# A gated recurrence and a dense block: when the weights of the second layer are converted, and where a unit's pairs stand

## The chip, the cores and the metric

The kernel runs on one core of one Trainium2 chip. The metric is the device time of one execution in microseconds (us); less is better. Engines are named as the profile names them: PE is TensorE (PEld its weight loads), DVE is VectorE, ACT is ScalarE, POOL is GpSimd, SP is SyncE, which only issues transfers here.

## The reference

For 4 batches and 8 heads, a recurrence over 768 steps with a 48x48 complex state, and then a dense block with a squared ReLU on 3072 rows of 384:

```python
mag = np.sqrt(a_re * a_re + a_im * a_im)
scale = np.minimum(mag, 0.999) / (mag + 1e-06)
a_re_n, a_im_n = (a_re * scale, a_im * scale)
for t in range(S):
    ar, ai = (a_re_n[:, :, t, :, None], a_im_n[:, :, t, :, None])
    new_re = ar * S_re - ai * S_im
    new_im = ar * S_im + ai * S_re
    kv = np.einsum('bhd,bhe->bhde', k[:, :, t], v[:, :, t])
    S_re, S_im = (new_re + kv, new_im)
    y[:, :, t] = np.einsum('bhd,bhde->bhe', q[:, :, t], S_re)
...
x = y.transpose(0, 2, 1, 3).reshape(B * S, H * D)
h = x @ w_in            # 384 -> 2048
r = np.maximum(h, 0.0)
out = (r * r) @ w_out   # 2048 -> 384
```

## The kernel before, in words

The work is cut into 8 units: each of the 4 batches in two halves of 384 steps. The second half of a batch takes over the state of the first. A unit goes through four stages.

- **Chain** (chain_work: load, roots, normalise, inner, inverse, totals, scan, back, apply). The decays are normalised and their products over time formed, mostly on DVE with some steps on ACT. Each step works on the 8 heads in two halves, z = 0 and z = 1 (4 heads each). Three steps need PE: totals turns the last products round (tile tot, L770), and after the scan back turns the results round again (tile bk, L835); apply then multiplies q and k by them and writes the tile QK (L862). The K half of QK goes to DRAM and back (rows, L869; KC, L871) to get another layout. These transfers are issued by POOL, and so are the loads of units 2 to 7 (L643); the loads of units 0 and 1 are issued by SP.
- **Pairs** (pair_work: turn, keep, score, mix). For each of 4 pairs of heads: transposes of QK (tq, L890), copied by ACT (QKT, L891); products of k and v (kv, L917), which DVE adds up to states (St, S, L925 and L927); scores (sa, L900), which DVE masks (A, L902); and the outputs (ypair, L936 and L941), which ACT copies to yt (L944) and SP sends to their place in xT (L952).
- **First dense layer** (hidden, L971): 16 tiles h of 128x384, three matmuls each; each matmul is two records in the trace. ACT makes g of h in two operations (L976, L977). The tiles h and o have three PSUM buffers together.
- **Second dense layer** (project, L985): three tiles o with 16 matmuls each, copied by ACT and stored by SP (L991).

The weights arrive as 64-bit floating-point numbers and are converted in 32 pieces of 128x384, 16 of w_in (tile w1) and 16 of w_out (w2). fetch (L581) loads a raw piece; lower (L589, ACT) scales its low words; convert (L602, L606, L609, DVE) makes the 32-bit numbers, frees the buffer and fetches another piece. The raw pieces of w2 have five buffers. The first five are fetched by POOL at the start, the other eleven by SP, each when a buffer comes free. `after(x, y)` puts an instruction behind another in the order and adds no wait on a semaphore. The first operation of a conversion is put so behind a QK: of unit 0 for w1 and the first five pieces of w2, of unit 1 for the other eleven.

The order of the program is written out by hand at the end of fast_path: lists of steps are either run one after the other or merged, each list spread evenly over the merged one. A scheduler then sets the order of instructions on each engine from this order and the dependencies, and each engine runs its instructions in that order. The order of stages is:

1. the chain of unit 0, with the first fetches in it;
2. the pairs of unit 0, merged with the conversions of w1;
3. the fetches of five pieces of w2; then the chain of unit 1, then the first layer of unit 0;
4. the pairs of unit 1, merged with the conversions of w2; then the chain of unit 2;
5. for n = 1 to 7: both dense layers of unit n, merged with the pairs of unit n+1 and the chain of unit n+2. For n = 1 the second dense layer of unit 0 is put ahead of unit 1's. In the last two, checks of the inputs take the place of the chain.

At the end a flag is read; for inputs out of range a second, general path would run, which these inputs don't take.

Of the kernel before, what the change touches and what calls it, by code (L numbers as in the profile page):

```python
# [481 lines left out]
def fast_path(ctx, tc, q, k, v, a_re, a_im, moe_w_in, moe_w_out, out, flag):  # L482
# [21 lines left out]
    NF = FF // C  # L504
# [12 lines left out]
    NRAW = 5  # L517
# [9 lines left out]
    def after(x, y):  # L527

        tc.add_manual_dep(x.ins, y.ins.name, NOSYNC, reason="order")
# [14 lines left out]
    mark = {}  # L544
# [13 lines left out]
    def piece(i):  # L558
        words = 2 if wide else 1
        if i < NF:  # L560
            w_in = moe_w_in.bitcast(U32) if wide else moe_w_in
            return (w1[:, i].rearrange("p m f -> p (m f)"),
                    w_in[:, ts(i, words * C)].rearrange("(m p) f -> p m f", p=C))
        i -= NF
        w_out = moe_w_out.bitcast(U32) if wide else moe_w_out
        return w2[:, i], w_out[ts(i, C), :].unsqueeze(1)
# [4 lines left out]
    def fetch(i):  # L571

        dst, src = piece(i)
        if not wide:
            nc.gpsimd.dma_start(
                out=dst.rearrange("p (m f) -> p m f", m=src.shape[1]), in_=src)
            return

        raw = raws[i] = (gp.tile([C, DM, 2], U32, name="raw", tag="g") if i < NF else
                         wst.tile([C, DM, 2], U32, name="raw", tag="raw"))  # L580
        get = (nc.sync if i >= NF + NRAW else nc.gpsimd).dma_start(  # L581
            out=raw.rearrange("p (m f) two -> p m (f two)", m=src.shape[1]), in_=src)
        after(get, mark["landed"])

    def lower(i):

        if wide:
            lo = raws[i][:, :, 0]
            op = act.activation(out=lo, in_=lo, func=AF.Copy, scale=2.0 ** -29)  # L589
            after(op, mark["last"])  # L590

    def convert(i):

        for j in range(i, i + AHEAD) if i % NF == 0 else [i + AHEAD - 1]:
            if j // NF == i // NF:
                lower(j)
        if wide:
            dst, _ = piece(i)
            more, hi = raws[i][:, :, 0], raws[i][:, :, 1]
            bits = dst.bitcast(U32)  # L600

            first = dve.tensor_scalar(out=bits, in0=hi, scalar1=0x07FFFFFF, scalar2=3,  # L602
                                      op0=ALU.bitwise_and, op1=ALU.logical_shift_left)

            after(first, mark["QK", int(i >= NF + NRAW)])
            dve.scalar_tensor_tensor(out=bits, in0=hi, scalar=0xC0000000, in1=bits,  # L606
                                     op0=ALU.bitwise_and, op1=ALU.bitwise_or)

            dve.tensor_tensor(out=bits, in0=bits, in1=more, op=ALU.add)  # L609
        n = i + (NF // 2 if i < NF else NRAW)  # L610
        if n < (NF if i < NF else 2 * NF):
            fetch(n)
# [44 lines left out]
    def flat(t):  # L657
        return t.rearrange("p h c d -> p (h c d)")
# [86 lines left out]
    def measure_rest(u):  # L745
        for z in range(2):
            measure(u, 4 + z, whole(u["qk", z]))
        measure(u, 6, u["v"].rearrange("p j h d -> p (j h d)"))
# [90 lines left out]
    def apply(u, z):  # L839

        a, fa, fb, hs = u["a", z], u["fa", z], u["fb", z], ts(z, HH)
        xn, qk = u["xn"], u["qk", z]

        def over(j):
            return xn[:, j, hs].unsqueeze(2).to_broadcast([C, HH, W, D])

        dve.tensor_tensor(out=qk[:, 1], in0=qk[:, 1], in1=over(2), op=ALU.mult)
        for j, f in ((0, fa), (1, fb)):
            for r in range(2):
                dve.tensor_tensor(out=f[:, r], in0=a[:, r], in1=over(j), op=ALU.mult)  # L850
        dve.tensor_tensor(out=flat(a[:, 0]), in0=flat(fa[:, 0]), in1=flat(fb[:, 1]),
                          op=ALU.subtract)
        dve.tensor_tensor(out=flat(a[:, 1]), in0=flat(fa[:, 1]), in1=flat(fb[:, 0]),
                          op=ALU.add)
        t = pr.tile([C, 2 * HH * W * R], F32, name="QK", tag="QK")
        half = HH * W * R
        out_q = u["Q", z] = t[:, 0:half].rearrange("p (h c e) -> p h c e", h=HH, c=W)
        out_k = t[:, half:2 * half].rearrange("p (c h e) -> p c h e", h=HH, c=W)
        u["K", z] = out_k
        for j, o in ((1, out_k.rearrange("p c h e -> p h c e")), (0, out_q)):  # L860
            for r in range(2):
                done = dve.tensor_tensor(out=o[:, :, :, r * D:(r + 1) * D], in0=qk[:, j],  # L862
                                         in1=a[:, r], op=ALU.mult)
        mark["QK", u["n"]] = done

        rows = dram.tile([L, HH * R], F32, name="rows", tag=f"rows{z}")
        kc = u["KC", z] = nat.tile([C, NM, HH, R], F32, name="KC", tag=f"KC{z}")
        n = NM - u["half"]
        nc.gpsimd.dma_start(out=rows.rearrange("(p c) e -> p (c e)", c=W),  # L869
                            in_=out_k.rearrange("p c h e -> p (c h e)"))  # L870
        nc.gpsimd.dma_start(out=kc[:, 0:n].rearrange("p j h e -> p j (h e)"),  # L871
                            in_=rows.rearrange("(j p) e -> p j e", p=C)[:, 0:n])
# [7 lines left out]
    def turn(u, i, c):  # L880

        if c == 0:
            u.setdefault("T", {})[i] = pr.tile([R, 4, L], F32, name="QKT", tag="QKT")
        z = 2 * i // HH
        ps = bank(u, [R, 4, C], "tq", c == 1)
        for j in range(2):
            for h in range(2):
                hh = (2 * i + h) % HH
                src = u["K", z][:, c, hh] if j else u["Q", z][:, hh, c]
                nc.tensor.transpose(ps[:, 2 * j + h], src, ident)  # L890
        act.copy(out=u["T"][i].rearrange("r z (p c) -> r c z p", c=W)[:, c], in_=ps)  # L891
# [63 lines left out]
    def pair_work(u):  # L955
        w = []
        for i in range(NP):
            w += [[lambda i=i, c=c: turn(u, i, c)] for c in range(W)]
            if i:
                w += [[lambda i=i: keep(u, i - 1)], [lambda i=i: score(u, i, 0)],  # L960
                      [lambda i=i: mix(u, i - 1)], [lambda i=i: score(u, i, 1)]]
            else:
                w += [[]] + [[lambda h=h: score(u, 0, h)] for h in range(2)]
        w += [[lambda: keep(u, NP - 1)], [], [lambda: mix(u, NP - 1)], [], []]
        return [lambda fs=fs: [f() for f in fs] for fs in w]
# [27 lines left out]
    def hidden_work(u):  # L993
        return [lambda f=f: hidden(u, f) for f in range(NF)]

    def project_work(u):
        return [lambda c=c, p=p: project(u, c, p) for c in range(W) for p in range(4)]

    def chain_work(u):
        def both(*fs):  # L1000
            return [lambda z=z, f=f: f(u, z) for f in fs for z in range(2)]

        return ([lambda: load(u), lambda: None, lambda: None] + both(roots, normalise, inner, measure_roots, inverse)
                + [lambda j=j: totals(u, j) for j in range(3)]
                + [lambda: scan(u), lambda: measure_rest(u)]
                + [lambda j=j: back(u, j) for j in range(3)] + both(apply))
# [28 lines left out]
    def merge(*lists):  # L1035

        order = sorted((((i + 0.5) / len(w), n, i) for n, w in enumerate(lists)
                        for i in range(len(w))))
        for _, n, i in order:
            lists[n][i]()  # L1040

    units = [{"b": b, "half": half, "n": b * NHALF + half}
             for b in range(B) for half in range(NHALF)]
# [3 lines left out]
    merge(pair_work(units[0]), [lambda i=i: convert(i) for i in range(NF)])  # L1047
    for i in range(NF, NF + NRAW):
        fetch(i)
    for f in chain_work(units[1]) + hidden_work(units[0]):  # L1050
        f()
    merge(pair_work(units[1]), [lambda i=i: convert(i) for i in range(NF, 2 * NF)])
    for f in chain_work(units[2]):
        f()
    for n in range(1, NU):
        u = units[n]
        lists = [hidden_work(u) + project_work(u)]
        if n == 1:
            lists[0] = project_work(units[0]) + lists[0]
        if n + 1 < NU:  # L1060
            lists.append(pair_work(units[n + 1]))
        if n + 2 < NU:
            lists.append(chain_work(units[n + 2]))
        elif n + 1 < NU:
            lists.append([lambda i=i: inspect(i) for i in range(2 * NF)])
        else:
            lists.append([verdict])
        merge(*lists)
# [53 lines left out]
```

## Time and profile before

| what | value |
|---|---|
| median of 9 runs | 807.94 us (801.63 to 814.22) |
| the profiled execution's own time | 810.44 us |
| its span, first to last instruction | 808.6 us |
| mean granted PE clock in it | 0.969 of full speed |
| busy time of PE, DVE, ACT, POOL | 710.4, 518.9, 398.1, 109.9 us |
| HBM read, written | 56.62 MB, 14.16 MB |

Times in the profile are counted from the first instruction. A line of the order in time has the start, the time, the engine, the line of the kernel, the operation, the tiles out<-in, the shape and the count of instructions merged in it, and in brackets how long the engine was idle before it and what ended that. Each instruction's time overlaps a little with the next one's, so the distance from start to start is what counts. A matmul's time includes its way through the array.

### The profile page before, as it was taken

What the parts mean: (1) busy time and instruction counts of PE and PEld (TensorE: products, weight loads), DVE (VectorE), ACT (ScalarE), POOL (GpSimd) and SP (SyncE); (2) the same over time, 40 slices, a digit from 0 to 9 for tenths busy, and PEclk for the clock granted to TensorE, in tenths of its full rate; (3) what the DMA queues carried; (4) which work ended last, traced back from release to release, by engine and by line L of the source; (5) the groups of instructions that cost most, each with busy time, mean ns of one, the idle gap of its engine ahead of it and who ended that gap; (6) DMA issues with size and microseconds to landing.
All of it is one profiled execution on the core that took longest, in us unless ns stands there. A gap on an engine that the chain in (4) does not pass through costs nothing.

```text
span 808.6 us, 9895 instructions
## 1 busy us (share of the span) xinstructions
PE 710.4 (88%) x3474; PEld 463.8 (57%) x3474; DVE 518.9 (64%) x1332; ACT 398.1 (49%) x753; POOL 109.9 (14%) x162
## 2 busy tenths in 40 slices
PE   0138895599899999999999998999999999899997
PEld 0027553475466566666666665666666665566554
DVE  5897799987988985549582867378655957500000
ACT  5824495355478519931685139711982145212510
POOL 5003100410030023000500041002200144100000
PEclk9996898699999999999999999999999999899999
DMA  9428320551042035000800052003500278500000
GB/s 282 147 73 272 105 78 20 177 183 53 11 166 84 18 95 176 9 18 18 277 12 7 28 191 71 13 14 114 184 9 18 76 242 268 185 17 28 1 12 23
DMA packets 38747, 76.24 MB, mean 94 GB/s; under 512 B 10752, under 2 KB 25216, under 8 KB 38688
## 3 DMA queue, kind: packets, MB, share of 16 engines
q0 software_dynamic: 14608, 55.85, 21.3%
q1 hardware_dynamic: 24080, 19.67, 8.2%
q8 instruction: 29, 0.48, 0.2%
q14 instruction: 30, 0.25, 0.1%
HBM read 56.62 MB, written 14.16 MB: 88 GB/s over the span
## 4 chain that ended last, share of the span: by engine, by line
PE 28%; issue 27%; DVE 13%; DMA 10%; ACT 8%; POOL 2%; SPq 0%; POOLq 0%; ACTq 0%
PE o L985 15%; PE h L971 6%; DMA a<-in_a_im_dram 3%; DMA rows<-QK 2%; DVE fa L799 2%; DMA look<-in_moe_w_in_dram 2%; DMA look<-in_moe_w_out_dram 2%; PE sa L900 2%; DVE fa L706 2%; ACT QKT L891 1%; DVE a L694 1%; PE ypair L941 1%; PE ypair L936 1%; ACT g L976 1%; DVE QK L862 1%
## 5 line engine op out<-in xcount | busy, mean ns | idle before, releaser
L971 PE MATMUL h<-xT,w 128*128 128x384 f32 x768 | 269.1, 492 | 4.6 <-DMA xT<-yt 3.1
L985 PE MATMUL o<-w,g 128*128 128x384 f32 x768 | 264.9, 493 | 0.0
L985 PEld LDWEIGHTS o<-w,g 128*128 128x128 f32 x768 | 141.4, 192 | 85.7 <-issue 4.9
L971 PEld LDWEIGHTS h<-xT,w 128*128 128x128 f32 x768 | 139.0, 192 | 83.6 <-issue 6.2
L891 ACT COPY QKT<-tq 96x512 f32<-96x512 f32 x96 | 79.9, 855 | 36.0 <-PE tq L890 36.0
L976 ACT ACTIVATE g<-h 128x384 f32<-128x384 f32 x128 | 61.5, 484 | 54.8 <-PE h L971 54.7
L890 PE MATMUL tq<-ident,QK 128*96 128x128 f32 x384 | 61.3, 295 | 21.4 <-DVE QK L862 14.9
L890 PEld LDWEIGHTS tq<-ident,QK 128*96 128x96 f32 x384 | 47.9, 137 | 44.0 <-issue 27.3
L902 DVE TENSOR_TENSOR A<-sa,mask 128x384 f32<-128x384 f32 x64 | 35.3, 552 | 54.7 <-PE sa L900 54.6
L977 ACT ACTIVATE g<-g 128x384 f32<-128x384 f32 x128 | 66.5, 523 | 2.1
L944 ACT COPY yt<-ypair 112x384 f32<-112x384 f32 x32 | 15.3, 477 | 97.3 <-PE ypair L941 90.5
L900 PEld LDWEIGHTS sa<-QKT 96*128 96x128 f32 x384 | 53.2, 202 | 14.5 <-ACT QKT L891 4.3
L900 PE MATMUL sa<-QKT 96*128 96x128 f32 x384 | 57.8, 291 | 2.0 <-ACT QKT L891 2.0
L869 POOL DMA_DIRECT2D rows<-QK x16 | 9.1, 566 | 335.9 <-DVE QK L862 335.9
L989 ACT COPY ot<-o 128x384 f32<-128x384 f32 x24 | 11.4, 476 | 84.0 <-PE o L985 84.0
L862 DVE TENSOR_TENSOR QK<-qk,a 128x576 f32<-128x576 f32 x64 | 44.4, 751 | 0.0
L770 PE MATMUL tot<-ident,last 128*128 128x128 f32 x72 | 14.4, 303 | 29.5 <-ACT last L730 25.4
L917 PEld LDWEIGHTS kv<-v,KC 128*96 128x96 f32 x320 | 33.4, 176 | 12.0 <-DMA KC<-rows 3.8
L936 PE MATMUL ypair<-A,v 128*48 128x128 f32 x384 | 39.7, 290 | 0.2 <-ACT yt L944 0.2
L917 PE MATMUL kv<-v,KC 128*96 128x48 f32 x320 | 34.4, 258 | 4.7 <-DMA KC<-rows 3.3
L836 ACT COPY xn<-bk 128x384 f32<-128x384 f32 x24 | 11.1, 481 | 49.2 <-PE bk L835 49.2
L668 ACT ACTIVATE fa<-a 128x1152 f32<-128x1152 f32 x16 | 18.6, 1160 | 30.3 <-DMA a<-in_a_im_dram 25.2
(109 smaller groups left out, 889.0 us busy)
## 6 DMA issues: line engine op xcount, KB each, us to landing
rows<-QK POOLq DMA_DIRECT2D x16, 576.0 KB, 4.2
raw<-in_moe_w_in_dram POOLq DMA_DIRECT2D x16, 384.0 KB, 6.7
look<-in_moe_w_in_dram POOLq DMA_DIRECT2D x16, 384.0 KB, 4.5
look<-in_moe_w_out_dram POOLq DMA_DIRECT2D x16, 384.0 KB, 4.3
KC<-rows POOLq DMA_DIRECT2D x8, 576.0 KB, 5.8
out_dram<-ot SPq DMA_DIRECT2D x24, 192.0 KB, 1.9
raw<-in_moe_w_out_dram SPq DMA_DIRECT2D x11, 384.0 KB, 3.6
xT<-yt SPq DMA_DIRECT2D x48, 72.0 KB, 2.2
```

What stands on the lines that cost most here:

```text
L668: square = act.activation(out=whole(fa), in_=whole(a), func=AF.Square, accum_out=sums[:, n, z:z + 1])
L862: done = dve.tensor_tensor(out=o[:, :, :, r * D:(r + 1) * D], in0=qk[:, j], in1=a[:, r], op=ALU.mult)
L890: nc.tensor.transpose(ps[:, 2 * j + h], src, ident)
L891: act.copy(out=u["T"][i].rearrange("r z (p c) -> r c z p", c=W)[:, c], in_=ps)
L900: nc.tensor.matmul(sa[:, j], lhsT=T[:, 2 + h, ts(j, C)], rhs=T[:, h, ts(j, C)], start=True, stop=True)
L902: dve.tensor_tensor(out=u["A"][i][:, h], in0=sa, in1=mask3, op=ALU.mult)
L917: nc.tensor.matmul(ps[:, j, h], lhsT=u["KC", hh // HH][:, j, hh % HH], rhs=u["v"][:, j, hh], start=True, stop=True)
L936: nc.tensor.matmul(ypair[64 * h:64 * h + D, ts(j, C)], lhsT=u["v"][:, j, 2 * i + h], rhs=A[:, h, j], start=True, stop=S_j is None)
L971: nc.tensor.matmul(ps, lhsT=w1[:, f, m], rhs=u["xT"][:, m], start=(m == 0), stop=(m == NM - 1))
L976: act.activation(out=t, in_=ps, func=AF.Relu)
L977: act.activation(out=t, in_=t, func=AF.Square)
L985: nc.tensor.matmul(u["o"], lhsT=u["g"][f][:, ts(c, C)], rhs=w2[:, f], start=(f == 0), stop=(f == NF - 1))
```

## The change

All 16 pieces of w2 are now converted beside the first dense layer of unit 0, before the chain of unit 1 in the order. The second dense layer of unit 0 moves up beside the chain of unit 1, and the pairs of unit 1 stand alone, followed by the chain of unit 2. Every conversion is put behind the QK of unit 0 only. In the loop, the pairs of unit 2 (n = 1) get 30 empty steps ahead of their list before it is merged, so that they begin about half way through the dense layers of unit 1; those of unit 3 (n = 2) get 6. Units 4 to 7 are merged as before. Line numbers behind L605 are one lower in the changed kernel up to L863; those behind L864 are as before.

```diff
             first = dve.tensor_scalar(out=bits, in0=hi, scalar1=0x07FFFFFF, scalar2=3,
                                       op0=ALU.bitwise_and, op1=ALU.logical_shift_left)
-
-            after(first, mark["QK", int(i >= NF + NRAW)])
+            after(first, mark["QK"])
...
-        mark["QK", u["n"]] = done
+        if u["n"] == 0:
+            mark["QK"] = done
...
     merge(pair_work(units[0]), [lambda i=i: convert(i) for i in range(NF)])
     for i in range(NF, NF + NRAW):
         fetch(i)
-    for f in chain_work(units[1]) + hidden_work(units[0]):
-        f()
-    merge(pair_work(units[1]), [lambda i=i: convert(i) for i in range(NF, 2 * NF)])
-    for f in chain_work(units[2]):
+    merge(hidden_work(units[0]), [lambda i=i: convert(i) for i in range(NF, 2 * NF)])
+    merge(project_work(units[0]), chain_work(units[1]))
+    for f in pair_work(units[1]) + chain_work(units[2]):
         f()
     for n in range(1, NU):
         u = units[n]
         lists = [hidden_work(u) + project_work(u)]
-        if n == 1:
-            lists[0] = project_work(units[0]) + lists[0]
         if n + 1 < NU:
-            lists.append(pair_work(units[n + 1]))
+
+            late = {1: 30, 2: 6}.get(n, 0)
+            lists.append([lambda: None] * late + pair_work(units[n + 1]))
```

## Prediction

> **What bounds the kernel now.** I read the page first, then the time of each stage, then what TensorE waited for in the stages where it idles, then the order in time on TensorE and VectorE there.
>
> The page, with its span and first engine line:
>
> ```profile
> span 808.6 us, 9895 instructions
> PE 710.4 (88%) x3474; PEld 463.8 (57%) x3474; DVE 518.9 (64%) x1332; ACT 398.1 (49%) x753; POOL 109.9 (14%) x162
> ```
>
> TensorE (PE) is the bound on the whole, so 98 us of its idle time is what can be won. The stages (span, then busy time and count for PE, its weight loads, VectorE, ScalarE and GpSimd, granted clock, DMA share, GB/s):
>
> ```profile
> 102.00:128.30 26.30, 24.82 (x81) 14.24 (x81) 25.05 (x54) 25.11 (x54) 0.00 (x0) 1.00 0.22 73
> 128.30:150.00 21.70, 7.07 (x21) 3.75 (x21) 19.92 (x70) 5.99 (x14) 0.57 (x1) 0.70 0.00 1
> 150.00:180.00 30.00, 28.08 (x236) 22.73 (x237) 27.15 (x62) 16.34 (x27) 8.20 (x12) 0.93 0.73 239
> 180.00:304.00 124.00, 118.56 (x537) 73.59 (x536) 105.10 (x272) 68.17 (x128) 16.73 (x24) 0.99 0.23 72
> 304.00:389.00 85.00, 84.12 (x434) 55.58 (x433) 55.38 (x144) 45.96 (x90) 9.09 (x13) 1.00 0.20 63
> ```
>
> From 304 us PE is full and VectorE (DVE) has 30 us to spare per unit; PE alone counts there. Between 128 and 150 us it is the other way: PE idles 14.6 us, DVE is full. PE's waits from 102 to 305 us (us in total, times, longest):
>
> ```profile
> PE bk L835 <- DVE e L802: 10.8, 5, 5.6
> PE tq L890 <- DVE QK L862: 7.5, 1, 7.5
> PE h L971 <- DMA xT<-yt: 1.8, 1, 1.8
> ```
>
> So PE waits there for the chain of unit 1. The order in time on PE, at the first transposes (tq) of units 1, 2 and 3, and in a dense stretch:
>
> ```profile
> 150.03 3.83 PE L890 MATMUL tq<-ident,QK 128*96 128x128 f32 x17 [7.47 <-DVE QK L862]
> 179.33 18.97 PE L985 MATMUL o<-w,g 128*128 128x384 f32 x58
> 232.09 1.05 PE L890 MATMUL tq<-ident,QK 128*96 128x128 f32 x8
> 304.12 0.60 PE L890 MATMUL tq<-ident,QK 128*96 128x128 f32 x4
> ```
>
> At 150.03 PE waits although unit 0's whole second dense layer (o, 96 records) is undone: it is queued behind unit 1's pairs. 58 records in 18.97 us less the overlap of the last are 0.3225 us each, so that layer is 31.0 us. On DVE, one conversion of a weight piece (L602, L606, L609), and the ends of the chains of units 1, 2 and 3 (QK of the first half of the heads):
>
> ```profile
> 66.75 0.35 DVE L602 TENSOR_SCALAR w<-raw 128x384 uint32<-128x384 uint32 x1
> 67.02 0.55 DVE L609 CUSTOM_DVE_ANT_0 w<-raw,w 128x768 uint16<-128x768 uint16 x1
> 67.49 0.55 DVE L606 SCALAR_TENSOR_TENSOR w<-raw,w 128x384 uint32<-128x384 uint32 x1
> 67.96 0.35 DVE L602 TENSOR_SCALAR w<-raw 128x384 uint32<-128x384 uint32 x1
> ...
> 147.13 2.76 DVE L862 TENSOR_TENSOR QK<-qk,a 128x576 f32<-128x576 f32 x4
> ...
> 229.19 2.76 DVE L862 TENSOR_TENSOR QK<-qk,a 128x576 f32<-128x576 f32 x4
> ...
> 294.48 1.42 DVE L862 TENSOR_TENSOR QK<-qk,a 128x576 f32<-128x576 f32 x2
> ```
>
> From one L602 to the next a conversion takes 1.21 us. The QK ends are at 149.9, 232.0 and 295.9: a chain of a unit, beside the pairs of the one before and no conversions, takes 64 us of DVE's order.
>
> **The change, part by part.** The orders of both programs are alike up to about 97 us on each engine, and on PE again from the middle of unit 3's pairs on. I follow three marks, the first tq of units 1, 2 and 3, and compare at each the time and the dense work that PE has done by then.
>
> *Conversions of w2.* Before, 5 of the 16 lie inside unit 1's chain (98.7 to 121 us) and 11 in its pairs (158 to 178). After, DVE's order has all 16 in one run before the chain: 16 x 1.21 = 19.4 us after 97.6, so 117. Five raw pieces are there early (issued at 14.6 to 19.3). The other 11 each wait on SP for a buffer: SP issue 0.6, landing 3.6 (median of that row), ScalarE's L589 0.44 and its place among the g operations some 0.8, conversion 1.21, in all 6.7 us for a ring of five, against 6.05 of conversion. I add 1 us: 118 (117 if all lands in time; the slowest landing shown at this line, 9.0 us, gives up to 134, see the rivals). Behind these fetches on SP stand only unit 0's outputs, first due near 141, and unit 1's xT; unit 1's loads and unit 0's xT are ahead. POOL's order is unchanged. ScalarE has eleven L589 between unit 0's g operations; a piece not yet landed would hold the g behind it, and PE has three PSUM buffers of cover, 5.8 us.
>
> The Trainium skill, "DMA: Bandwidth & Descriptors", section "Anatomy of one DMA", speaks against so many waiting fetches on one queue: a wait is served on the issuing sequencer, so it holds what is behind. The same section's fit, 2.0 us and the bytes over 436 GB/s, would estimate 2.9 us for 384 KB, for GpSimd's path, and the run at 117; the row of 3.6 decides.
>
> *Unit 1's chain* starts at 118, not at 96.9. Without conversions it takes between 53.0 - 5 x 1.21 = 47 (unit 1's own) and 53.7 (unit 2's, 178.3 to 232.0); it shares ScalarE with six g pairs, so 52: QK at 170. But its transposes bk now stand behind unit 0's second layer on PE: 84 h records from 102.0 take 27.3, then 31.0 of o and 9 tot at 0.11, so 161.5. Three bk 0.8, ScalarE's copy 0.5, and 8.2 from there to QK (141.64 to 149.9): **QK at 171.2**, 21.3 later than before, and any chain start up to 119 gives the same. What PE does in exchange is 31.0 us of o. Ahead by 9.7 at the first mark. PE's idle stretch there shrinks from 14.6 to about 8 us and does not go; the slow first transposes (17 in 3.83 us against 0.11 each, some 2 us) are paid as before.
>
> *Unit 1's pairs and unit 2's chain.* The pairs end some 26 to 27.5 us after QK, as before without the o between; then h of unit 1 waits for the last xT as unit 0's did (98.1 to 102.0), which o covered before: 202. In DVE's order unit 2's L690 now stands behind the masks of pair 2 and L705 behind those of pair 3, so the first L705 comes 26 us after QK; from the same point (250.1 less two operations) to QK unit 3 took 45.8, less 5 for masks and St: 41. So 67.2, not 64: QK of unit 2 at 238.4. PE gets to that tq at about 237 after waits of some 4 at bk. Tq at 238.6. Before it was 232.1 with 27 of 48 h matmuls done; after, all 48 and 5 of o, 26 x 0.645 = 16.8 us more. Ahead by 10.3.
>
> *Unit 2's pairs, set 30 places later.* PE's order has 43 o matmuls (27.7) among them. Summed with tq 0.11, sa 0.67 for three, kv 1.0 for six, PE gets to unit 3's bk at 284; but DVE's order has unit 3's scan behind the St and masks of the second and third pair, whose matmuls come at 269 and 279, so e is ready at 288. A wait of 4. Then the rest of the pairs, 10 us, and the last xT again uncovered (2): 15 h matmuls done and tq of unit 3 at 307.3. Before it was 304.1 with none of those 15 (9.7 us). **Ahead by 6.5.** The 6 places of unit 3 move no more than this: bk of unit 4 has 2 us to spare by the same sum (13.3 us of PE from sa against 11.4 of DVE), so nothing.
>
> *The sum.* 808.6 - 6.5 = 802.1 span; the profiled execution took 810.44, 1.8 more than its span, so 804; it stood 2.5 above the median of the nine runs, 807.94. Predicted median: **801.5**. A measurement tells about 1% (8 us) from no change, so this is within it.
>
> **The rivals.**
> 1. *The two loops keep the 64 us of the trace* (for: that row is measured, and mine adds 3 and 4 us of in-order waits that I summed by hand; against: the masks do stand in that order). QK at 235.2 and 299.2, tq of unit 3 near 305: ahead by 9. With the waits at bk and xT covered too, 13 to 16. 797, down to 792. Chance 0.33.
> 2. *The stall only moves.* If unit 2's late kv and masks hold unit 3's scan 6 us longer, all 6.5 are gone: 808. For: DVE's idle time after would be above before's. Against: my sum already has 4 there. Chance 0.12.
> 3. *Slower: the raw pieces come late.* Eleven pieces through five buffers are three rounds; at the slowest landing of 9.0 each round is 5.4 longer, 16 us, less 1.2 of cover. Break-even is 7.7 us late, a landing of 6.2. For: POOL's raws had a median of 6.7. Against: DMA share is 0.22 there, and SP's median is 3.6. 809 to 816, say 811. Chance 0.10.
>
> **How the numbers follow.** My forecast has 0.45, own range 797 to 806. The bounds 792 and 812 leave out the far ends of rivals 1 and 3. Faster by over 1% (below 799.9): most of rival 1 (0.30) and a part of mine (0.08), 0.38. Slower by over 1% (above 816): 0.07, from rival 3 and the far end of 2. Within: 0.55.
>
> **What would show it.** Conversions of w2 in one run, ended near 118; no PE wait but some 8 us before unit 1's tq at about 171; tq of units 2 and 3 near 239 and 307; PE waits of about 4 for e at bk of units 2 and 3, and of 1 to 3 for xT. Wrong if the run ends after 126, if QK to QK takes 64 or 72, or if later units get new waits.

## The result, and the profile after

| | before | after |
|---|---|---|
| median | 809.04 us (55 runs, 800.4 to 815.85) | 819.16 us (18 runs, 811.4 to 825.68) |
| the profiled execution's own time; its span | 810.44; 808.6 | 816.83; 815.0 |

The ratio is 1.0132, 95% interval 1.0108 to 1.0156: the change makes the kernel 1.3% slower. The forecast was 801.5 us.

The page of the changed kernel, span and first engine line:

```profile
span 815.0 us, 9899 instructions
PE 711.6 (87%) x3474; PEld 463.9 (57%) x3474; DVE 521.2 (64%) x1332; ACT 400.0 (49%) x753; POOL 110.3 (14%) x162
```

Both engines are as busy as before (PE 710.4, DVE 518.9 us); what grew is the time in which PE does nothing. The stages of the changed kernel, in the same columns as before the change (span, then busy time and count for PE, its weight loads, VectorE, ScalarE and GpSimd, granted clock, DMA share, GB/s): the conversions; the chain of unit 1 beside o of unit 0; unit 1's pairs to unit 2's QK; from there to unit 3's QK:

```profile
97.00:117.00 20.00, 17.72 (x56) 10.29 (x55) 17.06 (x42) 14.41 (x32) 0.00 (x0) 1.00 0.72 233
117.00:174.30 57.30, 44.74 (x146) 26.31 (x144) 43.66 (x115) 25.22 (x50) 0.57 (x1) 0.90 0.03 11
174.30:244.10 69.80, 63.22 (x348) 43.16 (x348) 56.62 (x146) 46.75 (x87) 11.17 (x15) 0.94 0.25 80
244.10:310.80 66.70, 59.73 (x341) 38.81 (x340) 55.39 (x143) 33.88 (x58) 11.24 (x15) 1.00 0.29 94
```

In each of the last three PE idles 6.6 to 12.6 us and VectorE 11.3 to 13.6. Neither engine is full: each waits for the other. The order in time on PE:

```profile
99.75 27.33 PE L971 MATMUL h<-xT,w 128*128 128x384 f32 x84 [2.28 <-DMA xT<-yt]
126.91 18.22 PE L985 MATMUL o<-w,g 128*128 128x384 f32 x56
144.97 0.49 PE L769 MATMUL tot<-ident,last 128*128 128x128 f32 x3
145.30 2.75 PE L985 MATMUL o<-w,g 128*128 128x384 f32 x8
147.88 0.82 PE L769 MATMUL tot<-ident,last 128*128 128x128 f32 x6
148.54 10.49 PE L985 MATMUL o<-w,g 128*128 128x384 f32 x32
162.43 0.43 PE L834 MATMUL bk<-ident,e 128*128 128x128 f32 x2 [3.40 <-DVE e L801]
163.64 0.69 PE L834 MATMUL bk<-ident,e 128*128 128x128 f32 x2 [0.77 <-DVE e L801]
164.93 0.69 PE L834 MATMUL bk<-ident,e 128*128 128x128 f32 x2 [0.61 <-DVE e L801]
...
174.35 3.83 PE L890 MATMUL tq<-ident,QK 128*96 128x128 f32 x17 [7.47 <-DVE QK L861]
...
244.20 1.05 PE L890 MATMUL tq<-ident,QK 128*96 128x128 f32 x8
...
295.78 0.30 PE L834 MATMUL bk<-ident,e 128*128 128x128 f32 x1 [1.80 <-DVE e L801]
...
307.20 2.17 PE L971 MATMUL h<-xT,w 128*128 128x384 f32 x6
312.64 7.74 PE L971 MATMUL h<-xT,w 128*128 128x384 f32 x18 [3.27 <-DMA xT<-yt]
320.21 0.60 PE L890 MATMUL tq<-ident,QK 128*96 128x128 f32 x4
```

Two places matter. Unit 1's tot stands at 145 and 148, behind 28 and 32 matmuls of o. And the first tq of unit 3, at 320.21, stands behind h of unit 2 that waited 3.27 us for the last xT, though unit 3's QK was ready at 310.8. On VectorE, the first operation of the first piece of w2, the waits among the conversions and the last operation, then unit 1's chain:

```profile
93.36 0.36 DVE L602 TENSOR_SCALAR w<-raw 128x384 uint32<-128x384 uint32 x1
...
101.19 0.37 DVE L602 TENSOR_SCALAR w<-raw 128x384 uint32<-128x384 uint32 x1 [1.38 <-DMA raw<-in_moe_w_out_dram]
103.77 0.56 DVE L608 CUSTOM_DVE_ANT_0 w<-raw,w 128x768 uint16<-128x768 uint16 x1 [1.00 <-ACT raw L589]
111.38 0.36 DVE L602 TENSOR_SCALAR w<-raw 128x384 uint32<-128x384 uint32 x1 [0.55 <-DMA raw<-in_moe_w_out_dram]
116.88 0.56 DVE L608 CUSTOM_DVE_ANT_0 w<-raw,w 128x768 uint16<-128x768 uint16 x1
...
141.02 0.76 DVE L725 TENSOR_TENSOR qk<-qk,fb 128x576 f32<-128x576 f32 x1
148.74 1.23 DVE L774 TENSOR_TENSOR_SCAN x<-tot,x,mask 128x128 f32<-128x128 f32 x3 [6.96 <-PE tot L769]
```

The conversions end at 117.4, where they were forecast to end, with 2.9 us of waits. Then VectorE is through with its part at 141.8 and stands still for 6.96 us, until PE has come through the o matmuls to tot.

The marks of the prediction, the first tq of units 1, 2 and 3, with the dense work done by then counted in PE's time as in the prediction (31.0, 16.8 and 9.7 us):

| mark | before | forecast | after | ahead: forecast | ahead: after |
|---|---|---|---|---|---|
| unit 1 | 150.03 | 171.3 | 174.35 | +9.7 | +6.7 |
| unit 2 | 232.09 | 238.6 | 244.20 | +10.3 | +4.7 |
| unit 3 | 304.12 | 307.3 | 320.21 | +6.5 | -6.4 |
| end | 808.6 | 802.1 | 815.0 | +6.5 | -6.4 |

From the third mark to the end nothing more is won or lost in sum; the single units behind it differ by up to 2 us either way. One more thing enters the marks. Up to 97 us the two kernels have the same order, yet VectorE's last mask of unit 0 stands at different times, first in the kernel before, then in the changed one:

```profile
91.80 0.56 DVE L902 TENSOR_TENSOR A<-sa,mask 128x384 f32<-128x384 f32 x1 [1.61 <-PE sa L900]
```

```profile
88.24 0.56 DVE L902 TENSOR_TENSOR A<-sa,mask 128x384 f32<-128x384 f32 x1 [1.61 <-PE sa L900]
```

The profiled execution of the changed kernel had a head start of 3.6 us there. Add it, and it lost 10.0; the medians say 10.1. So near a hit is partly luck: for the other kernels below, the same sum lies between 0.5 us under and 6.4 us over the difference of the medians.

### The profile page after: what moved, and what is told of

It reads as the page before. It is cut to its first block, busy times and chain, and to the rows that moved or that the text cites. A ratio compares the mean times of both kernels' runs of the same rounds, so it can differ in the third digit from the quotient of the medians.

```text
span 815.0 us, 9899 instructions
## 1 busy us (share of the span) xinstructions
PE 711.6 (87%) x3474; PEld 463.9 (57%) x3474; DVE 521.2 (64%) x1332; ACT 400.0 (49%) x753; POOL 110.3 (14%) x162
## 4 chain that ended last, share of the span: by engine, by line
PE 37%; issue 21%; DVE 11%; DMA 10%; ACT 10%; POOL 1%; SPq 0%; ACTq 0%; POOLq 0%
PE o L985 17%; PE h L971 11%; DMA a<-in_a_im_dram 3%; DVE fa L798 2%; ACT QKT L891 2%; PE sa L900 2%; DMA look<-in_moe_w_in_dram 2%; DMA look<-in_moe_w_out_dram 2%; DMA xT<-yt 2%; PE kv L917 2%; PE tq L890 2%; PE ypair L936 2%; PE ypair L941 1%; DMA rows<-QK 1%; ACT g L976 1%
## 5 line engine op out<-in xcount | busy, mean ns | idle before, releaser
L971 PEld LDWEIGHTS h<-xT,w 128*128 128x128 f32 x768 | 141.5, 194 | 92.6 <-issue 15.2
L985 PEld LDWEIGHTS o<-w,g 128*128 128x128 f32 x768 | 141.4, 191 | 87.2 <-issue 4.5
L977 ACT ACTIVATE g<-g 128x384 f32<-128x384 f32 x128 | 66.4, 522 | 2.1
L989 ACT COPY ot<-o 128x384 f32<-128x384 f32 x24 | 11.4, 474 | 89.8 <-PE o L985 89.8
L653 POOL DMA_DIRECT2D v<-in_v_dram x18 | 15.9, 889 | 153.2 <-issue 136.1
L917 PE MATMUL kv<-v,KC 128*96 128x48 f32 x320 | 32.7, 251 | 4.3 <-DMA KC<-rows 2.6
L705 DVE TENSOR_TENSOR fa<-a 128x384 f32<-128x384 f32 x64 | 33.3, 552 | 0.3
```

The costliest lines, as they stand in the source:

```text
L705: dve.tensor_tensor(out=f, in0=a[:, :, :, c - 1], in1=a[:, j, :, c].unsqueeze(1).to_broadcast([C, 2, HH, D]), op=ALU.mult)
L917: nc.tensor.matmul(ps[:, j, h], lhsT=u["KC", hh // HH][:, j, hh % HH], rhs=u["v"][:, j, hh], start=True, stop=True)
L971: nc.tensor.matmul(ps, lhsT=w1[:, f, m], rhs=u["xT"][:, m], start=(m == 0), stop=(m == NM - 1))
L977: act.activation(out=t, in_=t, func=AF.Square)
L985: nc.tensor.matmul(u["o"], lhsT=u["g"][f][:, ts(c, C)], rhs=w2[:, f], start=(f == 0), stop=(f == NF - 1))
```

## The experiments

All ratios are to the kernel before, run on the same chip in the same job. "tq 1, 2, 3" are the marks in the profiled execution; h is the number of h matmuls of unit 2 ahead of the third.

| run | median | ratio (95%) | last mask of unit 0 ends | tq 1, 2, 3 (h) |
|---|---|---|---|---|
| before | 809.04 | 1 | 92.4 | 150.0, 232.1, 304.1 (0) |
| after | 819.16 | 1.0132 (1.0108 to 1.0156) | 88.8 | 174.4, 244.2, 320.2 (15) |
| e1 no empty places | 806.47 | 0.9988 (0.9952 to 1.0024) | 87.8 | 173.6, 243.5, 309.2 (10) |
| e2 empty places alone | 812.64 | 1.0039 (1.0002 to 1.0075) | 90.5 | 150.1, 236.4, 319.3 (15) |
| e3 tot earlier | 813.27 | 1.0043 (1.0005 to 1.0080) | 86.9 | 165.8, 238.3, 317.8 (15) |
| e4 e1 and e3 | 803.02 | 0.9928 (0.9890 to 0.9966) | 87.6 | 167.2, 239.2, 305.4 (10) |
| e5 12 places | 810.01 | 1.0008 (0.9975 to 1.0041) | 91.0 | 178.0, 246.3, 315.0 (10) |
| e7 conversions alone | 823.35 | 1.0185 (1.0129 to 1.0242) | 86.9 | 165.3, 232.2, 313.4 (0) |
| e8 the 30 places only | 816.70 | 1.0093 (1.0051 to 1.0134) | 88.3 | 174.0, 244.0, 318.9 (7) |
| e9 the 6 places only | 809.33 | 1.0004 (0.9971 to 1.0037) | 86.3 | 172.5, 242.1, 311.1 (15) |
| e10 e7, half the conversions | 814.89 | 1.0071 (1.0039 to 1.0104) | 90.8 | 162.2, 230.1, 311.5 (0) |
| e11 e7, PE's idle time filled | 821.48 | 1.0167 (1.0115 to 1.0218) | 86.3 | 165.8, 235.5, 317.1 (0) |
| e12 e4, chain 2 beside pairs 1 | 805.11 | 0.9956 (0.9923 to 0.9990) | 93.3 | 172.9, 239.3, 303.0 (0) |
| e13 e4, roots among conversions | 798.17 | 0.9912 (0.9880 to 0.9945) | 88.0 | 167.0, 239.3, 303.3 (10) |
| e14 after, unit 2's masks off VectorE | 812.56 | 1.0044 (1.0011 to 1.0076) | 87.2 | 173.3, 243.1, 306.2 (6) |
| e15 e1, unit 2's masks off VectorE | 805.81 | 0.9966 (0.9934 to 0.9999) | 89.6 | 176.4, 246.0, 310.2 (9) |

The kernel before had medians of 805.3 to 809.4 us in these jobs, so the ratios carry the verdicts.

### One part at a time: e1, e2, e3, e7

e1, the whole change without the empty places:

```diff
-            late = {1: 30, 2: 6}.get(n, 0)
+            late = 0
```

> The change without the empty places (pairs of units 2 and 3 merged from the first step, as before). Three theories. A: the late pairs are what costs (unit 2's masks and states hold unit 3's scan, and its last xT has no cover, so tq of unit 3 stands behind h that wait). B: unit 1's tot, queued on PE behind 28 to 32 matmuls of o, holds VectorE's scan 7 us, and this is passed on to the end. C: the 19.4 us of conversions ahead of unit 1's chain lie on the row of chains that VectorE sets, whatever the pairs do. By A: unit 1's tq stays at 174, unit 2's at 244, QK of unit 3 comes 64 us after that of unit 2 (308) and tq of unit 3 near 308 with only 3 h fewer done: 10 us gained, 809 us, as before (ratio 0.995 to 1.005). By B and C: nothing gained, 819 (1.010 to 1.016); with fewer o left for PE under the scan it can be some us worse.

Measured: 0.9988. A holds, B and C fail as an account of this part: the empty places cost 1.0132 - 0.9988, 1.4% or 11.6 us. The window from the second mark to the third, in e1 and in the changed kernel (columns as above):

```profile
243.50:309.20 65.70, 62.38 (x349) 40.40 (x349) 58.46 (x151) 36.05 (x64) 13.70 (x19) 0.98 0.35 112
```

```profile
244.20:320.20 76.00, 67.19 (x359) 43.09 (x359) 62.77 (x155) 38.39 (x67) 17.14 (x24) 0.98 0.38 122
```

PE is idle for 3.3 us in the one and 8.8 in the other. Two rows of e1 stand against those at 312.64 and 320.21 above: the last xT still leaves PE waiting, but 7.5 us earlier, and the first tq of unit 3 comes 3.0 us behind its QK (ready at 306.2) instead of 9.4 (ready at 310.8).

```profile
305.13 4.28 PE L971 MATMUL h<-xT,w 128*128 128x384 f32 x8 [2.36 <-DMA xT<-yt]
309.21 1.31 PE L890 MATMUL tq<-ident,QK 128*96 128x128 f32 x8
```

e2, the empty places in the kernel before and nothing else (the loop gets the same two lines as in the change):

> The kernel before with the empty places alone (30 ahead of unit 2's pairs, 6 ahead of unit 3's); conversions and the second layer of unit 0 stay. By A: up to the first tq of unit 2 as before (150 and 232); then unit 3's scan waits behind unit 2's late masks, the last xT is uncovered, and the end is 6 to 11 us later: 815 to 820 (1.007 to 1.014). By B and C: the late pairs cost nothing, 809 (0.997 to 1.003).

Measured: 1.0039, some 3 us. The sign is that of A, the size is not: 0.4% where A gave 0.7 to 1.4%. In its profiled execution 4.3 us are lost by the second tq, up to which the order is that of the kernel before (VectorE waited some 4 us longer for ScalarE, scores and raw pieces there), and only 1.2 between the second and the third, with the 15 h counted. PE still has the second layer of unit 0 in hand here beside unit 1's dense work. It fits that late pairs cost most where the dense work that could cover them has been used up before; no run tests this by itself.

e3, the whole change with tot and bk at other places among the o matmuls:

```diff
-    merge(project_work(units[0]), chain_work(units[1]))
+    p, w = project_work(units[0]), chain_work(units[1])
+    merge(p[:5], w[:13])
+    for f in w[13:16]:
+        f()
+    merge(p[5:10], w[16:18])
+    for f in w[18:21] + p[10:] + w[21:]:
+        f()
```

> The whole change, but unit 1's tot stands on PE behind 20 matmuls of o instead of 28 to 32, and bk behind 40 instead of 48. By B: VectorE's wait of 7 us for tot goes, QK of unit 1 comes at 167 to 168 instead of 174, and all that follows moves with it: 812 to 813 (1.004). By A: the first mark moves too, but from unit 2's pairs on their late place sets the end, so at most half is kept: 816 (1.009). By C: QK of unit 1 can't come before PE is through with h and o and VectorE through with the conversions; 3 us gained, 816.

Measured: 1.0043, 0.9% or 7 us under the whole change (5.9 by the medians). B's 812 to 813 against 813.3. As bk moves as well, this is the gain of both places and not the price of tot alone. VectorE in e3, the last operation of the inverse, the first products, and the scan on tot without a wait:

```profile
138.88 0.76 DVE L725 TENSOR_TENSOR qk<-qk,fb 128x576 f32<-128x576 f32 x1
139.71 0.93 DVE L798 TENSOR_TENSOR fa<-e 128x192 f32<-128x192 f32 x2
140.56 1.22 DVE L774 TENSOR_TENSOR_SCAN x<-tot,x,mask 128x128 f32<-128x128 f32 x3
```

and PE, where the last o matmuls now stand between bk and tq, so that the wait of 7.47 us for QK is 1.59:

```profile
137.80 0.82 PE L769 MATMUL tot<-ident,last 128*128 128x128 f32 x6
...
153.26 0.30 PE L834 MATMUL bk<-ident,e 128*128 128x128 f32 x1 [1.22 <-DVE e L801]
...
158.17 6.09 PE L985 MATMUL o<-w,g 128*128 128x384 f32 x14
165.84 2.44 PE L890 MATMUL tq<-ident,QK 128*96 128x128 f32 x18 [1.59 <-DVE QK L861]
```

e7, the kernel before with the conversions moved ahead of unit 1's chain and nothing else:

```diff
-    for f in chain_work(units[1]) + hidden_work(units[0]):
-        f()
-    merge(pair_work(units[1]), [lambda i=i: convert(i) for i in range(NF, 2 * NF)])
-    for f in chain_work(units[2]):
+    merge(hidden_work(units[0]), [lambda i=i: convert(i) for i in range(NF, 2 * NF)])
+    for f in chain_work(units[1]) + pair_work(units[1]) + chain_work(units[2]):
         f()
```

> The kernel before with the conversions of the second layer's weights moved ahead of unit 1's chain and nothing else: the second layer of unit 0 stays beside unit 1's dense work, no empty places. QK of unit 1 then comes at 165 to 168 instead of 150 with no more work done by PE. By C: these 15 to 18 us are not made good, 820 to 825 (1.014 to 1.02). By A and B: unit 1's pairs have no conversions to share VectorE with (13.3 us), so the loop to unit 2's QK is shorter than 82 by about as much, and the end comes 2 to 4 us later: 812 (1.002 to 1.006).

Measured: 1.0185, C's number. QK of unit 1 comes at 165, and PE's idle time is what was lost. First the stretch of unit 1's chain, then that from unit 2's QK to unit 3's:

```profile
117.00:165.20 48.20, 14.43 (x45) 7.75 (x43) 42.11 (x113) 22.11 (x44) 0.57 (x1) 0.61 0.00 0
...
232.10:305.30 73.20, 72.39 (x393) 48.35 (x394) 59.93 (x152) 43.49 (x84) 8.06 (x11) 1.00 0.23 77
```

PE idles 33.8 us in the first and is full in the second: VectorE catches up, PE can't. So A and B, which had unit 1's shorter pairs make it good, are wrong on this part. Together: the conversions ahead cost 1.0185; the second layer of unit 0 put into the idle time that they make wins 1.0185 - 0.9988, 2.0%; the empty places give back 1.4%.

### Do the conversions cost by their time, and does PE's idle time slow its clock? e10, e11

e10 is e7 with half of the pieces left out:

```diff
-    merge(hidden_work(units[0]), [lambda i=i: convert(i) for i in range(NF, 2 * NF)])
+    merge(hidden_work(units[0]), [lambda i=i: convert(i) for i in range(NF, NF + 8)])
```

> The kernel before with only 8 of the 16 pieces of the second layer's weights converted, all ahead of unit 1's chain; the other half is filled with a constant early on GpSimd and not loaded (this part of the weights is left out). It stands against the run with all 16 moved ahead and nothing else (823 us). By C, the time of the conversions ahead of the chain counts one for one: 9.7 us less of them, unit 1's QK at 155 instead of 165, the end 8 to 10 us earlier: 813 to 815 (1.005 to 1.008). If it is not their time but the order of the rest that costs there, the end moves by less than 3: 820 to 823.

Measured: 1.0071, 1.1% or 9 us under e7. In the profiled execution unit 1's QK is only 3.1 us sooner, but unit 0's pairs had ended 3.9 later; against those it is 7.0. By the medians the time of the conversions counts nearly one for one (9 of 9.7 us) when PE has nothing else to do; the two intervals leave some 5 us of doubt on the 9.

e7's profiled execution lost 8.5 us of span and its median 14.5. One guess was that PE's long idle time lowers its clock for what follows. e11 is e7 with 48 matmuls that nobody reads beside unit 1's chain:

```diff
+    def idle():
+        ps = dp.tile([C, DM], F32, name="idle", tag="d")
+        for f in range(4):
+            nc.tensor.matmul(ps, lhsT=units[0]["g"][f][:, ts(0, C)], rhs=w2[:, f],
+                             start=(f == 0), stop=(f == 3))
...
+    p, w = [idle] * 12, chain_work(units[1])
```

> The kernel before with the conversions of the second layer's weights ahead of unit 1's chain, as in the run that moved them alone (823.4 us, mean granted clock 0.9575 over its runs, kernel before 0.970), and with 48 matmuls that nobody reads (tile idle) on PE beside that chain, in the place that the second layer of unit 0 has in the whole change. They need no result of the chain and nothing needs theirs. If PE's idle time itself lowers the granted clock afterwards, and this is why that run's median is 14.5 us up where its profiled execution lost 8.5: the clock comes to 0.967 to 0.972 and the time falls to 815 to 818, although PE does 31 us more work. If the clock has nothing to do with it: 823 to 825, as that run, and a clock of 0.957.

Measured: 1.0167, 821.5 us, though the mean granted clock rose from 0.9575 to 0.982. The guess falls, and the stretch behind unit 1's QK shows it directly. First e7, then e11:

```profile
165.00:232.00 67.00, 62.27 (x354) 42.58 (x354) 56.38 (x146) 35.80 (x62) 11.18 (x15) 0.97 0.29 92
```

```profile
165.00:232.00 67.00, 60.57 (x344) 41.71 (x345) 53.66 (x143) 33.41 (x58) 10.81 (x15) 0.95 0.28 90
```

With the idle time the granted clock of that stretch is 0.97, with it filled 0.95. The idle stretch has a low clock itself (0.61 in the row above), which lowers the mean over the run and costs little, as hardly any work stands in it: the first 17 tq of unit 1 took 3.68 us in e7, and 18 took 2.43 in e11. The 14.5 may be the difference of starts again: e7's profiled execution had its last mask of unit 0 end at 86.9, that of before at 92.4; 8.5 and 5.4 make 13.9. But the same sum gives 19.8 for e11, whose medians differ by 13.4, so this isn't shown. A mean clock can be compared between executions of one kernel, not between kernels with different idle time.

### The empty places in parts: e8, e9, e5

e8 has `{1: 30}`, e9 `{2: 6}` and e5 `{1: 12}` in the place of `{1: 30, 2: 6}`.

> The whole change with the 30 empty places ahead of unit 2's pairs, and without the 6 of unit 3. If the 30 carry the cost: 816 to 819 (1.010 to 1.013), QK of unit 3 at 310 to 311. If the 6 carry a part (h of unit 2 stands ahead of the first tq of unit 3): that tq comes at 314 to 317 and the time is 811 to 815.

> The whole change with the 6 empty places ahead of unit 3's pairs, and without the 30 of unit 2. If the 30 carry the cost: 806 to 808 (0.996 to 0.999). If the 6 cost something of their own, 809 to 812.

> The whole change with 12 empty places ahead of unit 2's pairs instead of 30, and none ahead of unit 3's. If each place costs (the cost grows with how late the pairs stand): between 806.5 (none) and 816.7 (30), 809 to 812. If only pairs so late that unit 3's scan and the last xT are held cost anything: 805 to 808.

Measured: 1.0093, 1.0004 and 1.0008. The 30 carry the cost (1.05% over e1). Neither the 6 nor the 12 can be told from none: the intervals of e1, e5 and e9 overlap over most of their width. The cost grows with how late the pairs stand; whether it does so from the first place is open.

### By which way do the 30 places cost? e14, e15

Both leave the mask of unit 2 out (ScalarE copies the scores instead), e14 in the changed kernel, e15 in e1:

```diff
+        if u["n"] == 2:
+            act.copy(out=u["A"][i][:, h], in_=sa)
+        else:
+            dve.tensor_tensor(out=u["A"][i][:, h], in0=sa, in1=mask3, op=ALU.mult)
```

> The whole change, with the scores of unit 2 copied by ScalarE instead of masked by VectorE (the mask of this one unit is left out). It stands beside the next run, which has the same without the empty places. With the masks on VectorE the empty places cost 12.7 us (819.2 against 806.5). If they cost because VectorE has unit 2's masks ahead of unit 3's scan in its order, the cost falls to 4 to 7 between these two, and QK of unit 3 comes as long after that of unit 2 in both (within 1.5 us). If they cost on PE (the last xT without cover, products and h in a row ahead of the first tq of unit 3), the cost stays at 9 to 13 and PE's waits in unit 3's stage stay near 8 us here.

> The change without the empty places, with the scores of unit 2 copied by ScalarE instead of masked by VectorE (the mask of this one unit is left out). VectorE has 4.3 us less to do ahead of QK of unit 3. If VectorE's row sets the end with early pairs: 803 to 805 (806.5 before this edit). If PE does: 805 to 807.

Measured: 1.0044 and 0.9966. The cost of the empty places falls from 1.4% (11.6 us) to 0.8% (6.3 us). QK of the first half of the heads, units 2 and 3, on VectorE: the changed kernel, e1, e14, e15:

```profile
241.30 2.76 DVE L861 TENSOR_TENSOR QK<-qk,a 128x576 f32<-128x576 f32 x4
...
308.06 2.75 DVE L861 TENSOR_TENSOR QK<-qk,a 128x576 f32<-128x576 f32 x4
```

```profile
240.63 2.75 DVE L861 TENSOR_TENSOR QK<-qk,a 128x576 f32<-128x576 f32 x4
...
303.40 2.76 DVE L861 TENSOR_TENSOR QK<-qk,a 128x576 f32<-128x576 f32 x4
```

```profile
240.15 2.76 DVE L861 TENSOR_TENSOR QK<-qk,a 128x576 f32<-128x576 f32 x4
...
303.27 0.74 DVE L861 TENSOR_TENSOR QK<-qk,a 128x576 f32<-128x576 f32 x1
304.10 2.08 DVE L861 TENSOR_TENSOR QK<-qk,a 128x576 f32<-128x576 f32 x3
```

```profile
243.07 2.76 DVE L861 TENSOR_TENSOR QK<-qk,a 128x576 f32<-128x576 f32 x4
...
304.90 2.76 DVE L861 TENSOR_TENSOR QK<-qk,a 128x576 f32<-128x576 f32 x4
```

From end to end these are 66.75, 62.8, 63.3 and 61.8 us. So by the medians about half of the cost (5.3 of 11.6) is VectorE's order: unit 2's late masks stand ahead of unit 3's scan. The four intervals leave some 5 us of doubt on the 5.3, so the half is rough; the stretch from QK to QK, 3.5 us shorter in e14 than in the changed kernel, points the same way. The rest (6.3) stays with the masks gone, and where it arises isn't shown. In e14 PE comes to the first tq of unit 3 as its QK is ready (306.24, after a wait of 0.28), with 6 h ahead of it, and only then waits 2.10 us for the last xT, with 24 records of h behind that wait and ahead of the rest of unit 3's tq. At that mark e14 stands 4.0 us ahead of e15 with 3 h (1.9 us) fewer done, and at the end 6.2 behind (spans of 810.0 and 803.8). So in this pair of executions the loss lies behind the third mark, and no run takes it apart. The masks also take VectorE's time, and ScalarE has work more in both runs; the difference of the two runs is free of that as far as it is alike in them.

### What is left of the change: e4, e12, e13

e4 has the edits of e1 and of e3.

> The whole change without the empty places, and with unit 1's tot and bk earlier on PE (behind 20 and 40 matmuls of o). If the two causes lie one behind the other on the row of chains (A and B), their gains add: 806.5 - 5.9 = 800.6 (ratio 0.986 to 0.994), first tq of units 1, 2, 3 near 166, 236 and 302. If PE has become the bound behind unit 1's pairs once the pairs of unit 2 stand early, the 7 us of B only turn into waits of PE at the first tq of units 2 and 3: 805 to 807 (0.995 to 0.999).

Measured: 0.9928 (0.9890 to 0.9966), 0.7% faster than before. The gains add for the most part: by ratios 1.4% and 0.9% alone, 2.0% together.

e12 is e4 with `merge(pair_work(units[1]), w[:13])` for the first steps of unit 2's chain, w:

> The run with both repairs (no empty places, tot earlier, 803.0 us) with the first steps of unit 2's chain merged with the pairs of unit 1, where that run has them behind these pairs. There VectorE waits 8.5 us for scores and states of unit 1's pairs with the chain of unit 2 queued behind. If these waits set QK of unit 2: it comes 3 to 6 us sooner after QK of unit 1 than 71.9, and the time is 797 to 801 (0.985 to 0.990). If PE or ScalarE sets it by then, 802 to 805.

Measured: 0.9956, not told apart from e4. QK of unit 2 does come 66.4 us after that of unit 1 instead of 71.9, but QK of unit 1 stands 5.7 later in this execution, as unit 0's pairs ended 5.8 later, and the median doesn't show the gain. By the third mark e4 has done 10 h of unit 2 (6.5 us of PE) and e12 none: with these counted, and from the last mask of unit 0, only 1.7 us of the gain are left there.

e13 is e4 with the first steps of unit 1's chain among the conversions:

```diff
-    merge(hidden_work(units[0]), [lambda i=i: convert(i) for i in range(NF, 2 * NF)])
     p, w = project_work(units[0]), chain_work(units[1])
-    merge(p[:5], w[:13])
+    merge(hidden_work(units[0]), [lambda i=i: convert(i) for i in range(NF, 2 * NF)], w[:7])
+    merge(p[:5], w[7:13])
```

> The run with both repairs (803.0 us) with the first steps of unit 1's chain (roots and normalise) merged with the conversions instead of standing behind them. In the whole change VectorE waits 3 us for raw pieces among the conversions and about 2 us for ScalarE in these first steps; one can fill the other. If VectorE's row from the conversions to unit 1's QK sets the end, unit 1's QK comes 3 to 5 us sooner and the time is 798 to 801 (0.986 to 0.990). If PE with h and o of unit 0 ahead of bk sets it by then: 802 to 804 (0.991 to 0.995).

Measured: 0.9912 (0.9880 to 0.9945), the fastest kernel here, but its interval overlaps e4's nearly whole, and QK of unit 1 came no sooner (166.8 against 167.0). PE waits there for e as in e4, with 1.14 us at the first bk: what sets that stretch is not told by this run.

## Why the prediction was wrong, point by point

- **What bounds the kernel**: right. PE alone counts from the third mark on, VectorE and PE by turns before it, and the later units did not change in sum: from the third mark to the end 494.8 us after, and 504.5 less the 9.7 us of h before.
- **The conversions**: the end was right (117.4, forecast 117 to 118), the sum behind it was not. From the first L602 of w2 (93.36) the run took 24.1 us, where the forecast had 16 x 1.21 and 1 more, 20.4; it ended in time because it began some 4 us sooner than the 97.6 of the forecast, as unit 0's pairs ended sooner in this execution. Rival 3, late raw pieces, did not happen: 2.9 us of waits in all. The Trainium skill, "DMA: Bandwidth & Descriptors", section "Anatomy of one DMA", would estimate 2.9 us for a transfer of this size on GpSimd's path. The eleven on SP's queue landed in 4.0 us (median) in the changed kernel; the measurement decides.
- **Unit 1's chain**: the step that failed is "any chain start up to 119 gives the same", with tot entered as "9 tot at 0.11" of PE's time. That priced tot's own matmuls and not who waits for them. VectorE's scan stands behind tot, tot stands behind 28 to 32 o matmuls in PE's order, and the place of each in the merged list decides. VectorE lost 6.96 us. PE came to bk at 159.0, not 161.5, as its h began 2.3 us sooner than in the forecast (99.75 against 102.0); there it waited 3.40 for e, and 0.77 and 0.61 more at the next two bk. So the first mark, 3.0 us late, was missed by some 5.3 on equal terms, and these waits for e, behind the late scan, are 4.8 of them. e3 won 5.9 to 7.2 us, with tot and bk both earlier. The forecast asked what stands behind bk, and did not ask it for tot.
- **Unit 1's pairs and unit 2's chain**: from QK to QK 69.9 us, forecast 67.2. VectorE came to unit 2's inner products about when it was forecast to (199.58, 25.4 us behind QK, forecast 26). The term that was too small is the 41 from there to QK, taken over from unit 3's chain: it took 44.5. VectorE's work in it was less by about the 5 us that the forecast took off, but it waited 5.2 us, 3.7 of them for ScalarE (L689, L716), where unit 3's chain had waited 2.6 in the kernel before.
- **Unit 2's pairs, 30 places later**: the step that failed is "e is ready at 288. A wait of 4. Then the rest of the pairs, 10 us, and the last xT again uncovered (2)", which set tq of unit 3 68.7 us after that of unit 2. It took 76.0. Counted from that tq, bk got its e at 51.6 instead of 49.4; the rest of the pairs took 11.4 instead of 10; and the 12 h ahead of the third tq, with the wait for xT among them, 13.0 instead of 9.3 (the wait 3.27 instead of 2, and the 18 records behind it 7.57 instead of 5.8, at a granted clock of 0.57 from 312.6 to 316.0). The larger fault is that these late pairs were costed only as they stand and not against the same pairs standing early, where the whole stretch takes 65.7 with 5 h matmuls (3.2 us) fewer (e1). The forecast's own marks fall in this part, from 10.3 to 6.5; against the early pairs the loss would have stood out.
- **The rivals**: rival 1, loops of 64 us, is refuted for the change (69.9 and 66.8; without the empty places the second takes 62.8, e1). Rival 2, "the stall only moves" because unit 2's masks hold unit 3's scan, is what happened at the second place, for roughly half of its cost. Its price of 6 was near that half (5.3 by e14 and e15), but its 808 has neither the tot wait nor the rest of the cost of the late pairs. No rival had a chain step on PE behind o.
- **The sum**: 801.5 forecast, 819.2 measured. In the marks the three stretches were missed by 3.0, 2.6 and 7.3 us, in all the 12.9 between the forecast span of 802.1 and the 815.0 of the profiled execution; the rest of the 17.7 is the distance of the profiled executions from their medians. With both places mended (e4) it is 803.0. The credit for o in PE's idle time and the last wait of that stretch (7.47, forecast some 8) were about right; what the new order makes VectorE and PE wait for was not, and it turned 6 us of gain into 10 of loss.

## What to carry to other kernels

When dense work is moved in front of a chain on an in-order engine, list every step of the chain that this engine serves, not only the last, and ask of each who waits for it; a step that takes 1 us of PE can hold VectorE for 7. Work that is put later must be priced against the same work put early: here 30 empty places cost 1.05%, in part because the late masks hold what is queued behind them on the other engine. And of a change with three parts, try each: here one part lost 1.9%, the second won 2.0% and the third lost 1.4%.

## What the runs showed of the hardware

The executions of the kernel before take between 800 and 816 us, and within each kernel here an execution's time goes with its mean granted clock: the lower the clock, the longer the time (correlation -0.71 to -0.96). A part of the spread has a place. The pairs of unit 0, in the same order in every kernel, end between 86.3 and 93.3 us, and the granted clock from 62.8 to 86 us goes with it (correlation -0.95 over the 16 profiled executions). Four kernels, in the order before, after, e12, e11 (columns as above; the last masks end at 92.4, 88.8, 93.3 and 86.3):

```profile
62.80:86.00 23.20, 20.87 (x134) 17.55 (x132) 15.73 (x42) 8.06 (x15) 6.95 (x9) 0.63 0.78 251
```

```profile
62.80:86.00 23.20, 19.12 (x149) 16.40 (x150) 19.05 (x51) 11.33 (x20) 7.04 (x9) 0.82 0.80 257
```

```profile
62.80:86.00 23.20, 21.34 (x126) 17.95 (x127) 17.40 (x47) 7.56 (x14) 6.95 (x9) 0.58 0.78 254
```

```profile
62.80:86.00 23.20, 18.73 (x162) 15.38 (x161) 20.03 (x55) 11.93 (x20) 6.96 (x9) 0.93 0.80 260
```

At a clock of 0.58 to 0.63 the pairs end 6 to 7 us later than at 0.93. So one profiled execution compared with another can be off by that much before the change even begins, and it helps to count marks from the last mask of unit 0 as well. That isn't the whole of the spread: the spans so corrected still miss the differences of the medians by up to 6.4 us. The Trainium skill, "TensorE: Matmul & The Clock Gate", Part 1, says that the clock is halved after an idle window and that the window runs free, so the same kernel pays a different price from run to run. The rows here fit the halving: in the changed kernel the 17 tq behind a wait of 7.47 us took 3.83 us at a granted clock of 0.50, and in e3 18 behind one of 1.59 took 2.44 at 1.00. How long PE must idle they don't tell (in e12 18 took 4.05 at 0.50 behind a wait of 2.95), and that the window runs free no run here shows. The same section puts the price of the ramp under 1% of a typical span; here the spread of the end of one stage is 7.0 of some 809 us, 0.9%.
